# When the operands for the second token group are made, in a linear attention plus mixture-of-experts kernel on one core

## Chip, core and metric

One core of a Trainium2 chip runs the whole program. Its engines work side by side, each in the order of its own instruction list, and wait for one another by semaphores: PE (TensorE, matrix products; PEld is its weight load), DVE (VectorE), ACT (ScalarE), POOL (GpSimd) and SP (SyncE, which issues the DMAs). The metric is the device time of one execution in microseconds.

## The reference, cut to what matters

```
phi(x):  proj = x @ w_phi;  proj -= max|proj|;  return [exp(proj), exp(-proj)]
kv  = sum_s phi(k)_s v_s ;  z = sum_s phi(k)_s
attn = (phi(q) @ kv) / (phi(q) @ z + 1e-6)          # 4 batches, 8 heads, 576 tokens, width 64
x = attn as (2304 tokens, 512)
p = domain_probs / sum(domain_probs)
out = sum over 4 experts e of  p[:, e] * (relu(x @ w1[e]) @ w2[e])      # hidden width 1024
```

All is float32. Each matrix product on PE is made of three: both operands are split into a rounded part ("hi") and a remainder ("lo"), and lo*hi, hi*lo and hi*hi are added in PSUM.

## The kernel before, in words

**Work.** The attention runs over 16 pairs of heads (pair 15 is the last). The expert part runs over 48 units: a unit is two 128-wide slices of one expert's hidden width, for one group of tokens. Units 0 to 15 serve the first group (512 tokens, `first_units`, L623), 16 to 31 the second (1024 tokens), 32 to 47 the third (768 tokens). Units 16 to 47 (`strassen_unit`, L715) replace eight half-size products by seven, A to D, whose operands on the x side are B11, B21 (the x of the group's first half, already split) and T1, T2, T3, B22, T4, sums and differences of x blocks (`x_ops`, L664). A unit's second product is made of four tiles (eight in the second group) by `l2_tile` (L573); each ends with a DVE instruction "out" (L592) that adds the PSUM result into the output tile, and there are two PSUM buffers ("l"), so the third tile waits for the first tile's "out".

**Order.** The order in every engine's list is written out by the program. A heap holds functions with keys (`later`, L100); `tick` (L491) moves a clock on and runs what is due. From pair 4 on the attention of later pairs and the first group's units are interleaved. There a tick is one piece of three 128x512 matmuls on PE, and is worth 192/(256 x 0.88) = 0.852 of a key, from key 85 on. Unit 0 has 8 ticks and each later one 16: 8 for its own first product (L618), 8 for the second product of the unit before (L582). So unit 13 begins at tick 200 (key 255.5), unit 14 at 216, unit 15 at 232; the first group ends at tick 248 (key 296.4). Pair i's steps are listed in `STAGES` (L447) with keys 16i + offset: for pair 15 the last use of its inputs is at key 256 (L468), the denominators' reciprocal ("rec", L403) at 271.2, the multiplication by it (`x_mul`, L417, in place on the tile rb) at 276.9. `LAST` is 277. In the second group a tick is one product or tile, and the key moves by 1.

**The x operands before.** The second half of the second group's x lies in DRAM (xd), written by pairs up to 11. At key 280.7 (`to_late`, L883) the pool "att", which holds all attention tiles, is closed, and the pool "late" takes its place; `x_load` (L658) fetches 1 MB into the tile xr 1.5 ticks later. Then 32 functions are spread from 11 ticks on, 0.7 ticks apart: six DVE instructions make T1 = xr - hi - lo and T2 (L700 to L702), T2 is split (hi on ACT L685, lo on DVE L689), T1 is split (lo on POOL L689), two DVE instructions make T3 (L703), then T3 and B22 are split (lo on POOL), four DVE instructions make T4 (L704, L705), and it is split (lo on DVE). Each name stands for two instructions of 128x512, for the halves c = 0 and 1. Unit 16 issues a product only when its operand's functions have been issued (L782). In it, the four tiles of unit 15's second product all follow product A (L796).

**Beside them.** Units from 16 on need sums of weight blocks ("ws", four DVE instructions L522 to L525), their rounding on ACT (L541) and remainders on POOL (L549); weights of the second product are split by L506 (ACT) and L512 (POOL).

Of the kernel before, what the change touches and what calls it, by code (L numbers as in the profile page):

```python
# [11 lines left out]
F32 = mybir.dt.float32  # L12
F32R = mybir.dt.float32r
# [7 lines left out]
def kernel(  # L21
# [17 lines left out]
    P = 128  # L39
    B, NP = kq.shape[0], kq.shape[1]  # L40
    D = w_phi.shape[0]
    NF = w_phi.shape[1]
    S = kq.shape[3] // 2
# [4 lines left out]
    NPAIR = B * NP  # L48
# [5 lines left out]
    PER = 16  # L54
# [5 lines left out]
    COPY_ENG, COPY_ENG0 = "avvaaaa", "avaaaaa"  # L60
    LO_ENG, LO_ENG0, HI_ENG, HI_ENG0 = "vvvvgg", "vvvvgv", "vgg", "agg"

    XA_START, XA_GAP, XA_LATE, XA_LOAD = 11, 0.7, 3.7, 1.5
    FETCH = (12, 28, 40, 46)
    W_WAIT = (5.5, 4.0, 0, 3.5)

# [33 lines left out]
    def later(key, fn):  # L100
        heapq.heappush(queue, (key, next(count), fn))
# [5 lines left out]

    att_stack = ExitStack()
    ap_ = att_stack.enter_context(tc.tile_pool(name="att", bufs=2))
    wbd = ap_.tile([P, 2 * NF], F32, name="wbd", bufs=1)  # L110
    wbd_hi = ap_.tile([P, 2 * NF], F32R, name="wbd_hi", bufs=1)
    wbd_lo = ap_.tile([P, 2 * NF], F32R, name="wbd_lo", bufs=1)

    def v_tile(dtype, name, tag, mid):

        t = ap_.tile([P, 5, 192], dtype, name=name, tag=tag, bufs=2)
        nc.gpsimd.memset(t.bitcast(F32)[:, :, 64:P], mid)
        return t

# [10 lines left out]
    def load_pair(i, what):  # L130
        s = pairs[i]
        b, hp = divmod(i, NP)
        t0 = b * S
        if what == "kq":
            s.kq = [ap_.tile([P, 2 * S], F32, name="kq", tag="kq", bufs=2)]

            parts = ((0, 2 * P), (2 * P, 4 * P)) if i == 0 else ((0, 4 * P),)
            for a, z in (*parts, (S - 64, S), (S, S + 64), (S + 64, 2 * S)):
                to = a + {S - 64: 64, S: -64}.get(a, 0)
                nc.sync.dma_start(s.kq[0][:, to : to + z - a], kq[b, hp][:, a:z])  # L140
            return
        vsrc = v[t0 : t0 + S, hp * P : (hp + 1) * P]
        if s.split_kv:
            vraw = s.v = ap_.tile([P, 5, P], F32, name="vraw", tag="vraw", bufs=1)
            nc.sync.dma_start(vraw[:, 0:4, :], vsrc[0:512].rearrange("(t p) d -> p t d", p=P))
            for r0 in (0, 64):
                nc.sync.dma_start(vraw[r0 : r0 + 64, 4, :], vsrc[512:S])
            return
        s.v = (v_tile(F32, "v32", "vhi", 1.0),)
        nc.gpsimd.memset(s.v[0][0:64, 4, :], 0.0)  # L150
        for h in range(2):
            src, dst = vsrc[:, h * 64 : (h + 1) * 64], s.v[0][:, :, h * P : h * P + 64]
            nc.sync.dma_start(dst[:, 0:4], src[0:512].rearrange("(t p) d -> p t d", p=P))
            nc.sync.dma_start(dst[64:P, 4], src[512:S])
# [10 lines left out]
    def split_pair(i, what):  # L165
        s = pairs[i]
        if what == "v":
            if not s.split_kv:
                return
            hi, lo = v_tile(F32R, "vhi", "vhi", 1.0), v_tile(F32R, "vlo", "vlo", 0.0)  # L170
            for h in range(2):
                g, d = slice(h * P, h * P + 64), s.v[:, :, h * 64 : (h + 1) * 64]
                round_to(i, 2, hi[:, :, g], d)
                nc.gpsimd.tensor_tensor(
                    lo[:, :, g], d, hi[:, :, g].bitcast(F32), op=ALU.subtract
                )


            for h in range(2):
                g, d = slice(h * P, h * P + 64), s.v[0:64, 4, h * 64 : (h + 1) * 64]  # L180
                nc.gpsimd.tensor_scalar(lo[0:64, 4, g], d, 1.0, 0.0, op0=ALU.mult, op1=ALU.add)
            nc.gpsimd.memset(lo[0:64, 4, 64:P].bitcast(F32), 1.0)
            nc.gpsimd.memset(hi[0:64, 4, :].bitcast(F32), 0.0)
            s.v = (hi, lo)
            return
        if not s.split_proj:
            return
        raw = s.kq[0]
        sl = KSL if what == "k" else QSL
        n = sl.stop - sl.start  # L190
        hi = ap_.tile([P, n], F32R, name=f"{what}hi", tag=f"{what}hi", bufs=1)
        lo = ap_.tile([P, n], F32R, name=f"{what}lo", tag=f"{what}lo", bufs=1)
        round_to(i, "kq".index(what), hi, raw[:, sl])
        nc.gpsimd.tensor_tensor(lo, raw[:, sl], hi.bitcast(F32), op=ALU.subtract)  # L194
        setattr(s, what, (hi, lo))
# [19 lines left out]
    def proj_sub(i, what, c):  # L215

        s = pairs[i]
        g = 4 if c < 2 else 2
        n = g * NF
        m = ap_.tile([P, 4], F32, name="m", tag="m", bufs=4)  # L220
        psv = s.ps.pop((what, c))[:, :n].rearrange("p (g f) -> p g f", f=NF)
        nc.vector.tensor_reduce(m[:, :g], psv, axis=AX.X, op=ALU.max, apply_absolute_value=True)  # L222
        d = s.d[what, c] = ap_.tile([P, 512], F32, name="d", tag="d", bufs=3)
        nc.vector.tensor_tensor(  # L224
            d[:, :n].rearrange("p (g f) -> p g f", f=NF), psv,
            m[:, :g].unsqueeze(2).to_broadcast([P, g, NF]), op=ALU.subtract,
        )

    def exps(src, rows, g, n, split):

        if split:
            e = ap_.tile([P, 1024], F32, name="e", tag="e", bufs=2)
            hi = ap_.tile([P, 1024], F32R, name="ehi", tag="ehi", bufs=4)
        else:
            e = ap_.tile([P, 1024], F32, name="e32", tag="ehi", bufs=4)
        ev = e[rows, : 2 * g * n].rearrange("p (g s n) -> p g s n", s=2, n=n)
        nc.scalar.activation(ev[:, :, 0, :], src, AF.Exp)
        nc.scalar.activation(ev[:, :, 1, :], src, AF.Exp, scale=-1.0)
        if not split:
            return [e]  # L240
        sl = (rows, slice(0, 2 * g * n))
        nc.scalar.activation(hi[sl], e[sl], AF.Copy)  # L242
        return [hi, (e, sl)]
# [231 lines left out]
            later(PER * i + o, functools.partial(fn, i, *args))  # L475
    FIRST = PER * (NP - 1) + 37
    LAST = PER * (NPAIR - 1) + 37

# [2 lines left out]
    NU = NE * NFC // 2  # L483
    clock = Pair()
    weights = {}
    late = []

    def after(steps, fn, *args):
        later(clock.key + steps * clock.step, functools.partial(fn, *args))
# [25 lines left out]
    def s_sums(n):  # L515


        (raw,) = weights["w1", n]
        s = late[0].tile([P, 4, 256], F32, name="ws", tag="ws", bufs=1)
        a11, a12, a21, a22 = (raw[:, f, c * 256 : (c + 1) * 256] for f in range(2) for c in range(2))  # L520
        sub, tt = ALU.subtract, nc.vector.tensor_tensor
        tt(s[:, 0], a21, a22, op=ALU.add)  # L522
        tt(s[:, 1], s[:, 0], a11, op=sub)
        tt(s[:, 2], a11, a21, op=sub)
        tt(s[:, 3], a12, s[:, 1], op=sub)  # L525
        weights["w1", n] = (raw, s)
# [129 lines left out]
    )  # L656

    def x_load(x, first, nt, wait=0):  # L658
        raw = x.raw = late[0].tile([P, NP, 512], F32, name="xr", tag="xr", bufs=1)
        a = first * P  # L660
        src = xd[:, :, a : a + nt].rearrange("c p t -> p c t")
        after(wait, lambda: nc.sync.dma_start(raw[:, :, :nt], src))

    def x_ops(x):  # L664


        tt, sub, add = nc.vector.tensor_tensor, ALU.subtract, ALU.add
        b12, b22 = x.raw[:, 0:2, : x.nt], x.raw[:, 2:4, : x.nt]
        (hi1, lo1), (hi2, lo2) = ([t.bitcast(F32) for t in x.op[k]] for k in ("B11", "B21"))
        t = {"T3": b12, "B22": b22}  # L670

        def temp(name, c):
            if c == 0:
                t[name] = late[0].tile([P, 2, x.nt], F32, name=name, tag="tt", bufs=2)
            return t[name][:, c]

        parts = {}

        def hi(name, c):
            if c == 0:  # L680
                parts[name] = [
                    late[0].tile([P, 2, x.nt], F32R, name=f"{name}{k}", tag=f"{name}{k}", bufs=1)
                    for k in ("hi", "lo")
                ]
            nc.scalar.activation(parts[name][0][:, c], t[name][:, c], AF.Copy)  # L685
# [25 lines left out]
    def spread(ops, start, gap):  # L711
        for i, fn in enumerate(ops):
            after(start + gap * i, fn)
# [132 lines left out]
    with tc.manual_schedule():  # L846
# [26 lines left out]
        xa, xb = Pair(), Pair()  # L873
# [6 lines left out]
            }  # L880
        out1 = []

        def to_late():  # L883

            att_stack.close()
            late.append(ctx.enter_context(tc.tile_pool(name="late", bufs=1, reuse_waits="tile")))
            out1.append(late[0].tile([P, 4, DM], F32, name="out1"))
            x_load(xa, xa.first + 4, xa.nt, XA_LOAD)
            ops = x_ops(xa)
            spread(  # L890
                [fn for k in ("t", "T2", "T1", "t3", "T3", "B22", "t4", "T4") for fn in ops[k]],
                XA_START, XA_GAP,
            )

        later(LAST + XA_LATE, to_late)
        clock.key = FIRST
        clock.step = (LAST - FIRST) / (NU * (2 * NP + 2 * N0) * SPREAD)
        pend = first_units()
        clock.key = max(clock.key, LAST + XA_LATE)
        run_until(clock.key)  # L900
        clock.step = 1
        second_units(pend)


# [36 lines left out]
```

## Time and profile before

| what | value |
|---|---|
| median of 3 runs (lowest to highest) | 988.18 us (985.95 to 990.49) |
| the profiled execution, own time | 989.25 us |
| its span, first to last instruction | 987.5 us |
| mean granted TensorE clock | 0.993 of full speed |
| PE busy | 957.0 us (97%) |
| PEld busy | 823.0 us (83%) |
| DVE busy | 723.6 us (73%) |
| POOL busy | 582.2 us (59%) |
| ACT busy | 467.1 us (47%) |

The profiled execution is 1.07 us above the median. In the profile's view of 40 equal slices, PE is at 9 tenths nearly everywhere; after the first slice the lowest digits (8 and 7) are those of slices 16 and 17 of 40, where the first group of units gives way to the second. Starts and durations below are in us from the span's start; "[2.10 <-DVE out L592]" means that the engine had been idle for 2.10 us and that this instruction released it; "x2" that two like instructions were merged. In the views by stretch each engine has its busy time and, in brackets, its count of instructions; PEclk is the granted clock, 1.00 being full speed.

### The profile page before, as it was taken

To read this page: it belongs to the slowest core of one execution; us is meant where nothing else is said; L and a number is where in the kernel's file an instruction comes from. 1 tells how busy PE (TensorE), PEld (TensorE's weight loads), DVE (VectorE), ACT (ScalarE), POOL (GpSimd) and SP (SyncE) were. 2 spreads that over 40 slices of the span, in tenths; PEclk is the share of its full clock that TensorE was granted. 3 is DMA by queue.
4 is the path that set the end of the run, shared out by engine and by line. 5 is a ranking of instruction groups with operands and counts; after the bars stand their busy time and mean duration, and the time that the engine had idled before them with its cause. 6 is when DMAs were issued, how large, how long until landed. Compare 5 with 4: busy or idle time off the path is not lost. (4 is left out here: it accounts for less than half of the span.)

```text
span 987.5 us, 13367 instructions
## 1 busy us (share of the span) xinstructions
PE 957.0 (97%) x4871; PEld 823.0 (83%) x4871; DVE 723.6 (73%) x1026; ACT 467.1 (47%) x820; POOL 582.2 (59%) x487
## 2 busy tenths in 40 slices
PE   6999999999999998799999999999989999999998
PEld 5878888888888876688888888888878888888887
DVE  5588888898898757867666667668876667676764
ACT  4777666666676723424333333433434434343441
POOL 3588768778678345654555445544665565655651
PEclk9999999999999998999999999999999999999999
DMA  6433434334333243231121111221132221212211
GB/s 157 127 88 85 117 95 118 96 105 126 105 105 90 68 135 111 80 95 45 43 92 56 55 44 43 64 62 45 42 107 86 65 70 59 86 61 69 64 43 64
DMA packets 64273, 80.75 MB, mean 82 GB/s; under 512 B 20144, under 2 KB 29744, under 8 KB 64208
## 3 DMA queue, kind: packets, MB, share of 16 engines
q1 hardware_dynamic: 64208, 79.90, 27.2%
q8 instruction: 38, 0.62, 0.3%
q14 instruction: 27, 0.22, 0.1%
HBM read 72.40 MB, written 7.49 MB: 81 GB/s over the span
## 5 line engine op out<-in xcount | busy, mean ns | idle before, releaser
L592 DVE SCALAR_TENSOR_TENSOR out<-l,pr,out 128x512 f32<-128x512 f32 x270 | 200.5, 748 | 93.9 <-PE l L582 92.7
L582 PE MATMUL l<-w2hi,h_lo 128*128 128x512 f32 x576 | 227.8, 396 | 8.5 <-DVE out L592 8.4
L582 PE MATMUL l<-w2hi,h_hi 128*128 128x512 f32 x576 | 227.8, 395 | 0.0
L582 PE MATMUL l<-w2lo,h_hi 128*128 128x512 f32 x576 | 227.4, 395 | 0.0
L549 POOL TENSOR_TENSOR w1lo<-wraw,w1hi 128x512 fp32r<-128x512 f32 x64 | 78.2, 1242 | 99.7 <-ACT w1hi L541 62.0
L582 PEld LDWEIGHTS l<-w2hi,h_lo 128*128 128x128 f32 x576 | 109.1, 189 | 28.9 <-DVE out L592 11.2
L582 PEld LDWEIGHTS l<-w2hi,h_hi 128*128 128x128 f32 x576 | 109.1, 189 | 23.4
L582 PEld LDWEIGHTS l<-w2lo,h_hi 128*128 128x128 f32 x576 | 109.1, 189 | 17.5
L512 POOL TENSOR_TENSOR w2lo<-wraw,w2hi 128x1024 fp32r<-128x1024 f32 x48 | 116.3, 2423 | 11.5 <-ACT w2hi L506 7.9
L749 POOL TENSOR_TENSOR c<-u,s 128x512 f32<-128x512 f32 (+1 forms) x32 | 37.6, 1174 | 85.3 <-DVE u L736 85.3
L739 ACT ACTIVATE h_hi<-c 128x512 fp32r<-128x512 f32 (+1 forms) x96 | 54.9, 578 | 68.7 <-DVE c L736 67.7
L549 POOL TENSOR_TENSOR s_lo<-ws,s_hi 128x768 fp32r<-128x768 f32 x32 | 59.2, 1849 | 33.0 <-ACT s_hi L541 32.3
L765 ACT ACTIVATE c<-c 128x512 f32<-128x512 f32 (+1 forms) x32 | 18.5, 580 | 126.3 <-POOL c L749 126.3
L242 ACT ACTIVATE ehi<-e 128x1024 fp32r<-128x1024 f32 (+2 forms) x72 | 63.5, 882 | 2.3
L257 DVE TENSOR_TENSOR elo<-e,ehi 128x1024 fp32r<-128x1024 f32 x36 | 61.9, 1721 | 0.3 <-ACT ehi L242 0.2
L746 POOL TENSOR_TENSOR h_lo<-c,h_hi 128x512 fp32r<-128x512 f32 (+1 forms) x32 | 37.5, 1172 | 40.2 <-ACT h_hi L739 40.2
L194 POOL TENSOR_TENSOR klo<-kq,khi 128x640 fp32r<-128x640 f32 x15 | 27.2, 1815 | 49.7 <-ACT khi L163 15.7
L222 DVE TENSOR_REDUCE m<-proj 128x4 f32<-128x512 f32 (+1 forms) x80 | 50.5, 631 | 7.4 <-PE proj L210 6.8
L506 ACT ACTIVATE w2hi<-wraw 128x1024 fp32r<-128x1024 f32 x48 | 50.5, 1052 | 10.2 <-PE l L582 9.9
L736 DVE TENSOR_TENSOR u<-s,B 128x512 f32<-128x512 f32 (+1 forms) x32 | 19.9, 620 | 47.2 <-ACT s L733 24.1
L541 ACT ACTIVATE s_hi<-ws 128x768 fp32r<-128x768 f32 x32 | 27.1, 846 | 56.9 <-DVE ws L525 56.9
L224 DVE TENSOR_TENSOR d<-proj,m 128x512 f32<-128x512 f32 (+1 forms) x80 | 51.1, 638 | 3.6
(165 smaller groups left out, 2496.4 us busy)
## 6 DMA issues: line engine op xcount, KB each, us to landing
wraw<-in_w_dram SPq DMA_DIRECT2D x96, 512.0 KB, 3.9
kq<-in_kq_dram SPq DMA_DIRECT2D x31, 256.0 KB, 4.6
rb<-rec_d SPq DMA_DIRECT2D x32, 144.0 KB, 2.8
out_dram<-out SPq DMA_DIRECT2D x18, 256.0 KB, 2.0
vraw<-in_v_dram SPq DMA_DIRECT2D x12, 256.0 KB, 4.1
xd<-rb SPq DMA_DIRECT2D x8, 288.0 KB
xr<-xd SPq DMA_DIRECT2D x2, 768.0 KB
kq<-in_kq_dram SPq DMA_DIRECT2D x32, 32.0 KB, 3.3
```

The lines of the kernel that those rows point to most:

```text
L222: nc.vector.tensor_reduce(m[:, :g], psv, axis=AX.X, op=ALU.max, apply_absolute_value=True)
L224: nc.vector.tensor_tensor(d[:, :n].rearrange("p (g f) -> p g f", f=NF), psv, m[:, :g].unsqueeze(2).to_broadcast([P, g, NF]), op=ALU.subtract,)
L242: nc.scalar.activation(hi[sl], e[sl], AF.Copy)
L257: engine.tensor_tensor(lo[sl], e[sl], parts[0][sl].bitcast(F32), op=ALU.subtract)
L506: nc.scalar.activation(hi, raw, AF.Copy)
L512: nc.gpsimd.tensor_tensor(lo, raw, hi.bitcast(F32), op=ALU.subtract)
L549: nc.gpsimd.tensor_tensor(dst, src, hi.bitcast(F32), op=ALU.subtract)
L582: nc.tensor.matmul(ps, lhsT=l[:, f, j * P : (j + 1) * P], rhs=r[:, f, :], start=(f == 0 and k == 0), stop=(f == 1 and k == 2),)
L592: nc.vector.scalar_tensor_tensor(o, ps, p, o, op0=ALU.mult, op1=ALU.add)
L739: nc.scalar.activation(h[b][0][:, f, :nt], src, AF.Relu)
L746: nc.gpsimd.tensor_tensor(dst, src, hi.bitcast(F32), op=ALU.subtract)
L749: nc.gpsimd.tensor_tensor(temp("c22"), c["u3"], c["s5"], op=ALU.add)
```

## The change

A second pool for SBUF, "att_in", on the other side of the memory, takes those attention tiles that are last used by key 256: the projection's weights, kq, v, their parts, d and e. The pool is closed at key 256.1 (`LAST_IN`), and a pool "early" takes its place with xr, ws, the work tiles of T1, T2 and T4, and the parts of T1, T2 and T3. The load of xr is issued there, and the 20 functions of T1, T2 and T3 follow at keys 260.1, 261.1, ... 279.1, one per key. B22 and T4 stay in "late"; their 12 functions are issued from 0.5 ticks into unit 16 on, 0.45 ticks apart, a tick there being one key. (The diff leaves out five places where kq, vraw, the parts of k and q, d and e go from pool `ap_` to `ip_`, and nothing else.)

```diff
@@ -60,7 +60,7 @@
     COPY_ENG, COPY_ENG0 = "avvaaaa", "avaaaaa"
     LO_ENG, LO_ENG0, HI_ENG, HI_ENG0 = "vvvvgg", "vvvvgv", "vgg", "agg"
 
-    XA_START, XA_GAP, XA_LATE, XA_LOAD = 11, 0.7, 3.7, 1.5
+    X_IN, X_GAP, XA_START, XA_GAP, XA_LATE = 4, 1, 0.5, 0.45, 3.7
     FETCH = (12, 28, 40, 46)
     W_WAIT = (5.5, 4.0, 0, 3.5)
 
@@ -107,13 +107,17 @@
 
     att_stack = ExitStack()
     ap_ = att_stack.enter_context(tc.tile_pool(name="att", bufs=2))
-    wbd = ap_.tile([P, 2 * NF], F32, name="wbd", bufs=1)
-    wbd_hi = ap_.tile([P, 2 * NF], F32R, name="wbd_hi", bufs=1)
-    wbd_lo = ap_.tile([P, 2 * NF], F32R, name="wbd_lo", bufs=1)
+
+
+    in_stack = ExitStack()
+    ip_ = in_stack.enter_context(tc.tile_pool(name="att_in", bufs=2, side="right"))
+    wbd = ip_.tile([P, 2 * NF], F32, name="wbd", bufs=1)
+    wbd_hi = ip_.tile([P, 2 * NF], F32R, name="wbd_hi", bufs=1)
+    wbd_lo = ip_.tile([P, 2 * NF], F32R, name="wbd_lo", bufs=1)
 
     def v_tile(dtype, name, tag, mid):
 
-        t = ap_.tile([P, 5, 192], dtype, name=name, tag=tag, bufs=2)
+        t = ip_.tile([P, 5, 192], dtype, name=name, tag=tag, bufs=2)
         nc.gpsimd.memset(t.bitcast(F32)[:, :, 64:P], mid)
         return t
 
...
@@ -475,6 +479,7 @@
             later(PER * i + o, functools.partial(fn, i, *args))
     FIRST = PER * (NP - 1) + 37
     LAST = PER * (NPAIR - 1) + 37
+    LAST_IN = PER * (NPAIR - 1) + 16.1
 
 
 
@@ -483,7 +488,7 @@
     NU = NE * NFC // 2
     clock = Pair()
     weights = {}
-    late = []
+    early, late = [], []
 
     def after(steps, fn, *args):
         later(clock.key + steps * clock.step, functools.partial(fn, *args))
@@ -516,7 +521,7 @@
 
 
         (raw,) = weights["w1", n]
-        s = late[0].tile([P, 4, 256], F32, name="ws", tag="ws", bufs=1)
+        s = early[0].tile([P, 4, 256], F32, name="ws", tag="ws", bufs=1)
         a11, a12, a21, a22 = (raw[:, f, c * 256 : (c + 1) * 256] for f in range(2) for c in range(2))
         sub, tt = ALU.subtract, nc.vector.tensor_tensor
         tt(s[:, 0], a21, a22, op=ALU.add)
@@ -656,7 +661,7 @@
     )
 
     def x_load(x, first, nt, wait=0):
-        raw = x.raw = late[0].tile([P, NP, 512], F32, name="xr", tag="xr", bufs=1)
+        raw = x.raw = early[0].tile([P, NP, 512], F32, name="xr", tag="xr", bufs=1)
         a = first * P
         src = xd[:, :, a : a + nt].rearrange("c p t -> p c t")
         after(wait, lambda: nc.sync.dma_start(raw[:, :, :nt], src))
@@ -671,15 +676,16 @@
 
         def temp(name, c):
             if c == 0:
-                t[name] = late[0].tile([P, 2, x.nt], F32, name=name, tag="tt", bufs=2)
+                t[name] = early[0].tile([P, 2, x.nt], F32, name=name, tag="tt", bufs=2)
             return t[name][:, c]
 
         parts = {}
 
         def hi(name, c):
             if c == 0:
+                pool = (early if name in ("T1", "T2", "T3") else late)[0]
                 parts[name] = [
-                    late[0].tile([P, 2, x.nt], F32R, name=f"{name}{k}", tag=f"{name}{k}", bufs=1)
+                    pool.tile([P, 2, x.nt], F32R, name=f"{name}{k}", tag=f"{name}{k}", bufs=1)
                     for k in ("hi", "lo")
                 ]
             nc.scalar.activation(parts[name][0][:, c], t[name][:, c], AF.Copy)
@@ -880,18 +886,29 @@
             }
         out1 = []
 
+        xa_ops = {}
+
+        def to_early():
+
+            in_stack.close()
+            early.append(
+                ctx.enter_context(
+                    tc.tile_pool(name="early", bufs=1, side="right", reuse_waits="tile")
+                )
+            )
+            x_load(xa, xa.first + 4, xa.nt)
+            xa_ops.update(x_ops(xa))
+            fns = [fn for k in ("t", "T2", "T1", "t3", "T3") for fn in xa_ops[k]]
+            for i, fn in enumerate(fns):
+                later(LAST_IN + X_IN + X_GAP * i, fn)
+
         def to_late():
 
             att_stack.close()
             late.append(ctx.enter_context(tc.tile_pool(name="late", bufs=1, reuse_waits="tile")))
             out1.append(late[0].tile([P, 4, DM], F32, name="out1"))
-            x_load(xa, xa.first + 4, xa.nt, XA_LOAD)
-            ops = x_ops(xa)
-            spread(
-                [fn for k in ("t", "T2", "T1", "t3", "T3", "B22", "t4", "T4") for fn in ops[k]],
-                XA_START, XA_GAP,
-            )
-
+
+        later(LAST_IN, to_early)
         later(LAST + XA_LATE, to_late)
         clock.key = FIRST
         clock.step = (LAST - FIRST) / (NU * (2 * NP + 2 * N0) * SPREAD)
@@ -899,6 +916,7 @@
         clock.key = max(clock.key, LAST + XA_LATE)
         run_until(clock.key)
         clock.step = 1
+        spread([fn for k in ("B22", "t4", "T4") for fn in xa_ops[k]], XA_START, XA_GAP)
         second_units(pend)
 
 
```

## Rows read from the trace of the kernel before

**Rows 1.** Busy time by stretch, PE alone: stretch, busy (count), granted clock, DMA share, GB/s.
```profile
366.86:418.00 51.14, 40.19 (x154) 0.90 0.28 91
420.00:540.00 120.00, 120.00 (x531) 1.00 0.21 66
```

**Rows 2.** Timeline of PE: start, duration, line, what, idle time before and its releaser.
```profile
369.35 0.80 PE L582 MATMUL l<-w2hi,h_lo 128*128 128x512 f32 x1 [2.10 <-DVE out L592]
...
384.20 0.79 PE L582 MATMUL l<-w2hi,h_lo 128*128 128x512 f32 x1 [3.46 <-DVE out L592]
...
387.52 0.79 PE L582 MATMUL l<-w2hi,h_lo 128*128 128x512 f32 x1 [0.39 <-DVE out L592]
...
398.15 0.50 PE L582 MATMUL l<-w2hi,h_lo 128*128 128x512 f32 x1 [2.48 <-DVE out L592]
...
407.75 0.47 PE L787 MATMUL D<-T4hi,w1lo 128*128 128x512 f32 x1 [1.14 <-DVE u L736]
...
417.55 0.50 PE L787 MATMUL A<-x_hi,w1lo 128*128 128x512 f32 x1 [1.38 <-ACT s L733]
```

**Rows 3.** Busy time by stretch, PE alone, right behind three of these pauses.
```profile
368.90:372.50 3.60, 3.15 (x7) 0.55 0.84 244
384.00:389.80 5.80, 5.21 (x11) 0.50 0.29 90
398.00:401.00 3.00, 2.85 (x12) 1.00 0.47 170
```

**Rows 4.** Timeline of DVE, 379 to 403 us.
```profile
379.29 1.53 DVE L522 TENSOR_TENSOR ws<-wraw 128x256 f32<-128x256 f32 x1
...
382.80 0.68 DVE L700 TENSOR_TENSOR T<-xr,x_hi 128x512 f32<-128x512 f32 x1
383.40 0.74 DVE L592 SCALAR_TENSOR_TENSOR out<-l,pr,out 128x512 f32<-128x512 f32 x1
384.06 2.14 DVE L700 TENSOR_TENSOR T<-xr,x_hi 128x512 f32<-128x512 f32 x1
...
393.66 3.78 DVE L703 TENSOR_TENSOR xr<-xr 128x512 f32<-128x512 f32 x2
...
400.52 2.81 DVE L704 TENSOR_TENSOR T<-x_hi,T 128x512 f32<-128x512 f32 x2
```

**Rows 5.** Timeline of POOL, four instructions between 347 and 397 us.
```profile
347.60 2.39 POOL L512 TENSOR_TENSOR w2lo<-wraw,w2hi 128x1024 fp32r<-128x1024 f32 x1
...
353.12 2.41 POOL L512 TENSOR_TENSOR w1lo<-wraw,w1hi 128x1024 fp32r<-128x1024 f32 x1 [3.12 <-ACT w1hi L506]
...
383.83 1.82 POOL L549 TENSOR_TENSOR s_lo<-ws,s_hi 128x768 fp32r<-128x768 f32 x1 [1.57 <-ACT s_hi L541]
...
394.07 2.82 POOL L512 TENSOR_TENSOR w2lo<-wraw,w2hi 128x1024 fp32r<-128x1024 f32 x1
```

**Rows 6.** Timeline of DVE, 347 to 367 us.
```profile
347.76 0.48 DVE L295 TENSOR_SCALAR nd<-num,eps 128x256 f32<-128x256 f32 x1
349.19 2.20 DVE L422 TENSOR_TENSOR rb<-nd,rb 64x576 f32<-64x576 f32 x2 [0.94 <-DMA rb<-rec_d]
351.42 0.69 DVE L605 SCALAR_TENSOR_TENSOR h_lo<-l,h_hi 128x512 fp32r<-128x512 f32 x1
353.67 0.75 DVE L592 SCALAR_TENSOR_TENSOR out<-l,pr,out 128x512 f32<-128x512 f32 x1 [1.56 <-PE l L582]
...
358.44 0.21 DVE L403 RECIPROCAL rec<-den 128x9 f32<-128x9 f32 x1
...
366.00 2.51 DVE L422 TENSOR_TENSOR rb<-nd,rb 64x576 f32<-64x576 f32 x2 [0.68 <-DMA rb<-rec_d]
```

**Rows 7.** Timeline of SP: the last DMA issues before 345 us, and when the next follows.
```profile
334.86 0.34 SPq L398 DMA_DIRECT2D den<-den_d  x1
344.02 0.33 SPq L406 DMA_DIRECT2D rec_d<-rec  x1
```

**Rows 8.** The page's DMA issues: KB each, median us from issue to landing.
```profile
wraw<-in_w_dram SPq DMA_DIRECT2D x96, 512.0 KB, 3.9
```

**Rows 9.** Timeline of PE, 333 to 355 us: pair 15's last projection, unit 12's third tile.
```profile
333.58 0.28 PE L210 MATMUL proj<-wbd_hi,qhi 128*128 128x256 f32 x1
...
354.85 0.39 PE L582 MATMUL l<-w2hi,h_lo 128*128 128x512 f32 x1
```

More of the change, by code (lines that the diff above doesn't have):

```diff
@@ L134, in load_pair @@
         if what == "kq":
-            s.kq = [ap_.tile([P, 2 * S], F32, name="kq", tag="kq", bufs=2)]
+            s.kq = [ip_.tile([P, 2 * S], F32, name="kq", tag="kq", bufs=2)]
             parts = ((0, 2 * P), (2 * P, 4 * P)) if i == 0 else ((0, 4 * P),)
@@ L143, in load_pair @@
         if s.split_kv:
-            vraw = s.v = ap_.tile([P, 5, P], F32, name="vraw", tag="vraw", bufs=1)
+            vraw = s.v = ip_.tile([P, 5, P], F32, name="vraw", tag="vraw", bufs=1)
             nc.sync.dma_start(vraw[:, 0:4, :], vsrc[0:512].rearrange("(t p) d -> p t d", p=P))
@@ L190, in split_pair @@
         n = sl.stop - sl.start
-        hi = ap_.tile([P, n], F32R, name=f"{what}hi", tag=f"{what}hi", bufs=1)
-        lo = ap_.tile([P, n], F32R, name=f"{what}lo", tag=f"{what}lo", bufs=1)
+        hi = ip_.tile([P, n], F32R, name=f"{what}hi", tag=f"{what}hi", bufs=1)
+        lo = ip_.tile([P, n], F32R, name=f"{what}lo", tag=f"{what}lo", bufs=1)
         round_to(i, "kq".index(what), hi, raw[:, sl])
@@ L222, in proj_sub @@
         nc.vector.tensor_reduce(m[:, :g], psv, axis=AX.X, op=ALU.max, apply_absolute_value=True)
-        d = s.d[what, c] = ap_.tile([P, 512], F32, name="d", tag="d", bufs=3)
+        d = s.d[what, c] = ip_.tile([P, 512], F32, name="d", tag="d", bufs=3)
         nc.vector.tensor_tensor(
@@ L231, in exps @@
         if split:
-            e = ap_.tile([P, 1024], F32, name="e", tag="e", bufs=2)
+            e = ip_.tile([P, 1024], F32, name="e", tag="e", bufs=2)
             hi = ap_.tile([P, 1024], F32R, name="ehi", tag="ehi", bufs=4)
```

## The prediction, made before the result was known

> **What bounds the kernel now.** I read the page first: PE is busy 97% of the span, so a change elsewhere pays only where PE stands still. The busy time by stretch says where that is. From 420 to 540 us, in the steady second group, PE issues 531 matmuls in 120 us, 0.226 us each; from 366.86 to 418.00, where the first group ends, it issues 154 in 51.14 us [rows 1]. At 0.226 us those need 34.8 us, so 16.3 us are lost there, and this is all that a change of this passage can win. Next the timeline of PE: six pauses, 2.10, 3.46, 0.39, 2.48, 1.14 and 1.38 us, 10.95 us together, four of them ended by a DVE "out" [rows 2]. Behind two of them the granted clock is 0.55 and 0.50, which is the lower of its two levels (1.2 GHz), for 3.60 and 5.80 us; behind the pause of 2.48 us it is 1.00 [rows 3]. At the lower level half of the busy time is loss: 1.6 and 2.6 us. The remaining 1.1 us is the refilling of PE after the pauses.
>
> Then the timeline of DVE says why "out" is late. The pause until 384.20 ends after the "out" of 383.40, which stood behind the weight sums from 379.29 and one T1 instruction at 382.80; the pause until 398.15 follows the two T3 instructions, 3.78 us [rows 2, 4]. DVE instructions with two SBUF inputs vary here from 0.68 to 2.14 us for the same size [rows 4]. POOL explains it: the one of 384.06 took 2.14 us while POOL worked from 383.83 to 385.65, so it ended 0.55 us after POOL did [rows 4, 5]. The two halves of x_mul from 349.19 took 2.20 us, and POOL was busy until 349.99 [rows 5, 6]. So such a DVE instruction waits until the POOL instruction in hand is over. "out" and h_lo, which read PSUM, keep to 0.69 to 0.75 us [rows 6].
>
> The Trainium skill, "SBUF — State Buffer", section "Who interferes with whom", has the rule: a DVE instruction with two SBUF inputs and a GpSimd instruction that reads SBUF exclude each other, and whichever came first holds the other off entirely. That speaks against this change, which moves such DVE work to a place with long POOL instructions. The trace agrees for DVE; for POOL it shows 2.82 us instead of 2.41 beside T3's two instructions [rows 5], a delay.
>
> **The change part by part.** *The load.* xr takes the place of the projection's weights and kq, whose last reader, pair 15's last projection, starts at 333.58 [rows 9]. It goes into SP's list behind the issue at 334.86 and ahead of the one at 344.02 [rows 7], so SP, idle in between, can issue it at about 335.5 and nothing queued behind it waits. 512 KB land in 3.9 us [rows 8]; 1 MB needs 3.9 (if latency were all) to 7.8 us (twice the bytes). I take 7.8, landed by 343.5; the first T1 instruction comes after 347.76 [rows 6]. Cost 0; if the cover were gone, see the third rival.
>
> *Twenty instructions in pair 15's time.* Keys 260.1, 261.1, ... are ticks 206, 207, 208, 209, 211, 212 for T1 and T2, that is the end of unit 13's first product and the first tiles of unit 12's second. Ten of the twenty run on DVE, six on ACT, four on POOL. The steps of a T instruction and an "out" are, from start to start, 0.60 and 0.66 us [rows 4]. Now DVE's list: nd ends at 348.24; T1 c0 waits for POOL until 349.99 and ends at 350.6; x_mul, 1.4 us without POOL (2.20 less the 0.80 that it waited), 352.0; T1 c1, 352.6; h_lo, 353.2 [rows 5, 6]. POOL has begun w1lo at 353.12 and holds until 355.53 [rows 5]. T1's second step c0 and c1 are both ahead of "out" (tick 209 lies inside the first tile): 356.1 and 356.7, "out" at 357.4, which before was over at 354.42 [rows 6]. PE wants to begin the third tile at 354.85 [rows 9] and begins at 357.5: **a new pause, +2.65 us.** At the least, if DVE's pair slips past w1lo, it is +0.4; at the most POOL comes between the pair, again about 2.7.
>
> *The reciprocal.* Behind it DVE has T2 c0, "out", T2 c1, "out", the first T2 remainder, the fourth tile's "out" (PE ends that tile at 360.2, the "out" at 361.2), the second remainder, then rec: 361.8 instead of 358.44 [rows 6], 3.4 later, of which 2.65 is PE's own shift. Rec starts the DMA chain to x_mul at 366.00, and x_mul stands ahead of the "out" that ended the pause of 2.10 us [rows 2, 6]. **+0.7 us** (0 to 1.7, the latter if T3's subtraction waits for T1's remainder on POOL). ACT's six and POOL's four instructions lie where those engines have idle time; POOL delays weights used 15 us later. Cost 0 there; without that cover it would be one POOL instruction, 1.8 us [rows 5].
>
> *Taken away from 380 to 399.* The pause of 3.46 loses one T1 instruction, **-0.6**; the weight sums stay ahead of "out", so 2.9 remains (bounds: 0 to 0.6, nothing else there is moved). The pause of 0.39 goes with the T1 instruction of 2.14, **-0.4**. T3's 3.78 leave the pause of 2.48, but the four T4 instructions, issued at keys 298.7 to 300.05 of unit 16, now stand between the first and second "out" of unit 15's tiles. Before, two of them took 2.81 us [rows 4]. From the start a of product A the first tile ends at a+2.7, "out" at a+3.4, the four T4 at a+5.8 without POOL or a+7.2 with B22's remainders on it, the second "out" at a+6.5 to a+7.9, and the fourth tile is due at a+5.4. The pause becomes 1.1 to 2.5; I take 2.1, as POOL has work there: **-0.4**. The pause of 1.14 waits for u behind T4's first remainder, which is now earlier: **-0.6** (0 to 1.1). The pause of 1.38 is ACT's and stays.
>
> *The clock.* The new pause, 2.65, lies between 2.48 (no drop) and 3.46 (drop); nearest is 2.48, so I take 0 and keep 1.6 [rows 3] for the range.
>
> **Sum:** 2.65 + 0.7 - 0.6 - 0.4 - 0.4 - 0.6 = +1.35 us. On the profiled execution's 989.25 that is 990.6; that execution lies 1.07 above the median of 988.18, so the forecast for a median is **989.5 us**: pauses change places. By the page's rule in both directions POOL would be held off as well and T3's remainders would come about one instruction later before x_mul: +0.6, 990.1.
>
> **The rivals.** *One: DVE's pair slips past POOL and the passage gets shorter.* T1's pair escapes w1lo (0.1 us decides), rec is not late, and the pause at 384.20, now 2.9, no longer drops the clock: +0.4 - 0.6 - 0.4 - 2.6 - 0.6, and between -1.0 and -2.48 for the T3 pause: -4.8 to -6.3, about 982.6. For it: DVE has idle time of 0.94 and 1.56 in that stretch [rows 6]. Against: w1lo starts at 353.12 and lasts 2.41 [rows 5].
>
> *Two, slower: the clock.* If a pause of 2.65 is enough (one of 2.10 was [rows 2, 3]), the new pause costs 1.6 more; the T4 pause, at its 2.5 and with a drop as well, 0.4 + 1.9 more: +1.35 + 1.6 + 2.3 = +5.3, 993.4. It decides from a pause of some 2.1 to 2.6 us on.
>
> *Three: the load is late.* If xr has to wait for tiles that POOL reads until 347.60, it lands at 355.4 and DVE stands at T1 c0 with x_mul, h_lo and "out" queued behind: "out" at about 360.9, 3.5 later than in the forecast: +4.9, 993.0, and SP's issue of 344.02 [rows 7] would be held too. Against: the tiles freed first are the first to be used again.
>
> **How the numbers follow.** Forecast 0.55, rival one 0.25, two 0.15, three 0.05. A measurement of this kernel tells 0.5%, 4.9 us, from no change. Rival one lies beyond it (faster 0.25), two and three at or beyond it (slower 0.20), the forecast, whose own bounds taken together give 985 to 992, within it (0.55). The range, 982 to 994, reaches to the middle of rival one and takes in two and three.
>
> **What would show it.** Right: the same six or so pauses, a new one before unit 12's third tile (about 355 to 357.5) ended by "out", a T1 instruction of over 2 us beside w1lo, rec near 362, the pause before unit 14's third tile still near 3 us, no T instruction between 383 and 399 but T4's. Wrong: no pause at 355; the stretch from 366.86 on losing well under 12 us; xr landing after 348; or new pauses after 420, where I expect none.

## The result, and the profile after

The changed kernel takes **999.13 us** (median of 4 runs, 996.98 to 999.87), the kernel before, beside it on the same chip, 988.78 (4 runs, 985.95 to 990.49): a ratio of 1.0097, 95% interval [1.0071, 1.0122]. It is slower by 10.35 us, twice what a measurement can tell, where 989.5 had been forecast with a range of 982 to 994. Median and range are both missed.

The profiled execution is one of 999.87 us, 10.62 above the profiled one of before. Its page, the span, the engines' busy times and the granted clock by slice:

```profile
span 998.1 us, 13366 instructions
...
PE 963.6 (97%) x4871; PEld 826.2 (83%) x4871; DVE 724.3 (73%) x1026; ACT 467.2 (47%) x820; POOL 583.9 (58%) x487
...
PEclk9999999999999998899999999999999999999999
```

The work is the same: 4871 matmuls, DVE and POOL within 2 us of before. PE alone is busy 6.6 us longer, and a second slice has a lower clock. The timeline of PE after shows its pauses in the passage, in the form of [rows 2] (start, duration, idle time before and its releaser):

```profile
360.92 0.79 PE L587 MATMUL l<-w2hi,h_lo 128*128 128x512 f32 x1 [2.19 <-DVE out L597]
...
377.27 0.50 PE L587 MATMUL l<-w2hi,h_lo 128*128 128x512 f32 x1 [1.98 <-DVE out L597]
...
391.57 0.75 PE L587 MATMUL l<-w2hi,h_lo 128*128 128x512 f32 x1 [2.86 <-DVE out L597]
...
406.39 0.79 PE L587 MATMUL l<-w2hi,h_lo 128*128 128x512 f32 x1 [4.75 <-DVE out L597]
...
427.04 0.50 PE L793 MATMUL A<-x_hi,w1lo 128*128 128x512 f32 x1 [1.16 <-ACT s L739]
```

And PE by stretch right behind the first four, the columns as in [rows 3]:

```profile
360.00:363.50 3.50, 2.58 (x6) 0.63 0.05 10
376.00:381.00 5.00, 3.73 (x10) 0.70 0.15 59
391.00:396.00 5.00, 4.43 (x12) 0.66 0.30 105
406.00:412.00 6.00, 5.61 (x13) 0.50 0.53 157
```

The first pause is the new one that the prediction named, and it has a lower clock behind it. The fourth, where 2.1 us had been expected, is 4.75, with 13 matmuls at the lower clock. The pauses that ended at 387.52 and 407.75 before are gone.

**The account.** Both programs issue the same 4871 matmuls in the same order, so each can be put beside its like and its start in the one execution taken from that in the other. This shift, how much later the kernel after is, grows as follows, in us; the times are those of before unless marked as now:

| where | forecast | measured |
|---|---|---|
| 53 to 60 us, long ahead of the changed passage | 0 | +3.7 |
| new pause ahead of unit 12's third tile | +2.65 | +2.4 |
| clock behind it | 0 | +1.7 |
| rec later, x_mul ahead of "out" (pause now at 377.27) | +0.7 | +0.2 |
| pauses of 384.20 and 387.52, and the clock behind them | -1.0 | -2.0 |
| pause of 398.15, now at 406.39 | -0.4 | +2.3 |
| clock behind it | 0 | +2.7 |
| pauses of 407.75 and 417.55 | -0.6 | -1.5 |
| **the passage** (all lines so far but the first) | **+1.35** | **+5.8** |
| 420 to 726 us, no pause added | 0 | +2.3 |
| 726 us to the end, a clock drop in the kernel before alone | 0 | -1.2 |
| **whole** | **+1.35** | **+10.6** |

Five places make up most of the difference; the timelines show what happened at each. *T4.* First DVE, then POOL of the kernel after:

```profile
398.96 0.75 DVE L597 SCALAR_TENSOR_TENSOR out<-l,pr,out 128x512 f32<-128x512 f32 x1 [1.99 <-PE l L587]
399.63 2.70 DVE L710 TENSOR_TENSOR T<-x_hi,T 128x512 f32<-128x512 f32 x2
402.25 3.42 DVE L711 TENSOR_TENSOR T<-T,x_lo 128x512 f32<-128x512 f32 x2
405.60 0.74 DVE L597 SCALAR_TENSOR_TENSOR out<-l,pr,out 128x512 f32<-128x512 f32 x1
```

```profile
398.80 2.99 POOL L695 TENSOR_TENSOR B22lo<-xr,B22hi 128x512 fp32r<-128x512 f32 x2 [5.16 <-ACT B22hi L691]
401.74 2.78 POOL L517 TENSOR_TENSOR w2lo<-wraw,w2hi 128x1024 fp32r<-128x1024 f32 x1
```

POOL is busy without a break from 398.80 to 404.52, and the four T4 instructions, between two "out", need 6.1 us. Before, w2lo ran at 394.07 [rows 5], ahead of B22 and T4; the change issues B22's functions at unit 16's start, so in POOL's list the weights' remainder now stands behind them. Its own input, w2hi, was done at 397.32 on ACT, while POOL stood idle until 398.80 for B22hi.

*The new pause.* DVE and POOL after, at unit 12's second product:

```profile
351.87 2.40 DVE L706 TENSOR_TENSOR T<-xr,x_hi 128x512 f32<-128x512 f32 x1
354.20 1.53 DVE L426 TENSOR_TENSOR rb<-nd,rb 64x576 f32<-64x576 f32 x2
...
356.97 3.23 DVE L707 TENSOR_TENSOR T<-T,x_lo 128x512 f32<-128x512 f32 x2
360.12 0.74 DVE L597 SCALAR_TENSOR_TENSOR out<-l,pr,out 128x512 f32<-128x512 f32 x1
```

```profile
351.32 2.41 POOL L517 TENSOR_TENSOR w2lo<-wraw,w2hi 128x1024 fp32r<-128x1024 f32 x1
...
356.66 2.39 POOL L517 TENSOR_TENSOR w1lo<-wraw,w1hi 128x1024 fp32r<-128x1024 f32 x1 [2.93 <-PE num L377]
```

T1's second step starts 0.3 us behind the start of w1lo, and the "out" behind it comes late, as forecast.

*The early part* lies where the change touches no instruction's order. The first fence is DVE before, the second DVE after, the third POOL after:

```profile
52.69 0.75 DVE L422 TENSOR_TENSOR rb<-nd,rb 64x576 f32<-64x576 f32 x1 [0.62 <-DMA rb<-rec_d]
53.60 1.19 DVE L422 TENSOR_TENSOR rb<-nd,rb 64x576 f32<-64x576 f32 x1 [0.16 <-DMA rb<-rec_d]
```

```profile
53.72 4.60 DVE L426 TENSOR_TENSOR rb<-nd,rb 64x576 f32<-64x576 f32 x2 [1.21 <-DMA rb<-rec_d]
```

```profile
55.36 2.33 POOL L517 TENSOR_TENSOR w2lo<-wraw,w2hi 128x1024 fp32r<-128x1024 f32 x1
```

The DMA that x_mul waits for landed about 1 us later, so the second half was still in hand when unit 1's w2lo began, and it ended after w2lo did. Before, it was over by 54.8.

*From 420 to 726.* The pace of the matmuls themselves differs. PE after: six products on x, six on T2 and the next tile's first, each run's first line:

```profile
440.84 0.39 PE L793 MATMUL A<-x_hi,w1lo 128*128 128x512 f32 x1
...
442.20 0.39 PE L793 MATMUL B<-T2hi,s_lo 128*128 128x512 f32 x1
...
443.60 0.39 PE L587 MATMUL l<-w2hi,h_lo 128*128 128x512 f32 x1
```

The same in the kernel before:

```profile
431.28 0.39 PE L787 MATMUL A<-x_hi,w1lo 128*128 128x512 f32 x1
...
432.64 0.39 PE L787 MATMUL B<-T2hi,s_lo 128*128 128x512 f32 x1
...
434.00 0.39 PE L582 MATMUL l<-w2hi,h_lo 128*128 128x512 f32 x1
```

On x: 1.36 us for six in both, 0.227 each. On T2: 1.40 after (0.233) and 1.36 before. No pause shows it; the count of matmuls in a long stretch does. The first line is before, the second after:

```profile
440.00:700.00 260.00, 260.00 (x1149) 1.00 0.19 57
```

```profile
440.00:700.00 260.00, 260.00 (x1139) 1.00 0.19 59
```

Ten matmuls fewer in 260 us, at a full clock and no idle time.

*From 726 on.* Ahead of the third group's first product PE pauses equally long in both executions. Only the kernel before has the lower clock behind it. The pause and the stretch behind it, first before, then after:

```profile
726.27 0.44 PE L787 MATMUL A<-x_hi,w1lo 128*128 128x384 f32 x1 [2.56 <-ACT s L733]
```

```profile
726.00:730.00 4.00, 3.73 (x13) 0.71 0.58 223
```

```profile
738.09 0.44 PE L793 MATMUL A<-x_hi,w1lo 128*128 128x384 f32 x1 [2.55 <-ACT s L739]
```

```profile
737.80:741.80 4.00, 3.71 (x19) 1.00 0.60 231
```

So 1.5 us of the comparison go the other way, with no work of the change in it.

### The profile page after: what moved, and what is told of

Read it like the earlier page. It is cut to its first block, busy times and chain, and to the rows that moved or that the text cites. A ratio compares the mean times of both kernels' runs of the same rounds, so it can differ in the third digit from the quotient of the medians.

```text
span 998.1 us, 13366 instructions
## 1 busy us (share of the span) xinstructions
PE 963.6 (97%) x4871; PEld 826.2 (83%) x4871; DVE 724.3 (73%) x1026; ACT 467.2 (47%) x820; POOL 583.9 (58%) x487
## 5 line engine op out<-in xcount | busy, mean ns | idle before, releaser
L198 POOL TENSOR_TENSOR klo<-kq,khi 128x640 fp32r<-128x640 f32 x15 | 27.2, 1812 | 49.5 <-DMA wraw<-in_w_dram 13.7
```

## The experiments

The theory taken into them: the slowdown is made of DVE held up by POOL at two places (T1's second step, T4), the clock behind those pauses, and the place of T1 to T3 in SBUF. The rivals: that the new pool or the earlier load costs by itself, that a late T1 would only move the wait, and that the place is innocent. Ratios are against the kernel before, with its median from the runs that shared the chip.

**The two pools alone.** The operands' functions and the load go back to where they were; the pools stay, and with them the place of T1 to T3's parts within 4096 bytes.

```diff
-            x_load(xa, xa.first + 4, xa.nt)
-            xa_ops.update(x_ops(xa))
-            fns = [fn for k in ("t", "T2", "T1", "t3", "T3") for fn in xa_ops[k]]
-            for i, fn in enumerate(fns):
-                later(LAST_IN + X_IN + X_GAP * i, fn)
...
+            x_load(xa, xa.first + 4, xa.nt, 1.5)
+            ops = x_ops(xa)
+            spread(
+                [fn for k in ("t", "T2", "T1", "t3", "T3", "B22", "t4", "T4") for fn in ops[k]],
+                11, 0.7,
+            )
...
-        spread([fn for k in ("B22", "t4", "T4") for fn in xa_ops[k]], XA_START, XA_GAP)
```

> The two pools as in the changed kernel, but the load of xr and all 32 functions issued where the kernel before issues them. Theory A (the loss is made of pauses and lower clock between 355 and 412 us; the 3.7 us that the changed kernel is already late at 60 us are chance in the arrival of DMAs): within 2 us of the kernel before, about 988 to 991. Theory B (the tiles' new places cost time wherever they are used): about 4 to 5 us over the kernel before, 993, with the 3.7 us at 60 us there again.

Measured: 991.35 us (10 runs), before 989.82; ratio 1.0033 [1.0012, 1.0053]. In its profile the passage costs 0.3 us, the early part is late as in the changed kernel, and the stretch of 440 to 700 us holds 1139 matmuls again. The time is as theory A had it, the late early part as theory B. So the pools cost about 1.5 us (1.2 to 5.2 by the interval) without any operand being made earlier, and the slow pace comes with them, not with the order. The greater part of the 10 us is the order's. The profiled execution is the slowest of the ten, 996.04, 4.7 us above their median: what it shows of the early part need not hold for the others.

**T4 behind the tiles.** Unit 15's tiles all come first, then B22 and T4.

```diff
-    X_IN, X_GAP, XA_START, XA_GAP, XA_LATE = 4, 1, 0.5, 0.45, 3.7
+    X_IN, X_GAP, XA_START, XA_GAP, XA_LATE = 4, 1, 6.3, 0.45, 3.7
```

> The changed kernel with XA_START 6.3 in place of 0.5, so that the four T4 instructions on DVE come behind the fourth out of unit 15's tiles. Theory A: the pause of 4.75 us and the 2.4 us at the lower clock behind it go, and at most 1 us comes back before product D; 5 to 7 us less than the changed kernel, 992 to 994. Rival (the pause belongs to something else, such as the weights' remainder on POOL): pause and time as in the changed kernel, 998 to 1000.

Measured: 990.4 us (10 runs); 1.0006 [0.9985, 1.0027]. One constant gives back 8.7 us: the pause near 400 is gone, and the passage is 3.6 us shorter than before the change. Behind the pause at 361 the clock stayed up here, although the edit comes 30 us after it. Pause and stretch in this kernel:

```profile
360.95 0.50 PE L587 MATMUL l<-w2hi,h_lo 128*128 128x512 f32 x1 [2.48 <-DVE out L597]
```

```profile
360.50:363.50 3.00, 2.55 (x11) 1.00 0.06 7
```

A pause of 2.48 us without a drop, where one of 2.19 had it in the kernel after: in this region the length alone does not decide, and in the profiled executions 1.7 us of the gain are not this edit's doing.

**T4 where it is, POOL out of its way.** This tells whether T4's four instructions are too many for their place or POOL makes them so: B22 goes behind the tiles, unit 16's w2lo is cut into four, T4 stays.

```diff
+        if kind == "w2" and n == 16:
+            for f in range(2):
+                for z in (slice(0, 256), slice(256, 512)):
+                    nc.gpsimd.tensor_tensor(
+                        lo[:, f, z], raw[:, f, z], hi[:, f, z].bitcast(F32), op=ALU.subtract
+                    )
+        else:
...
-        spread([fn for k in ("B22", "t4", "T4") for fn in xa_ops[k]], XA_START, XA_GAP)
+        spread([fn for k in ("t4", "T4") for fn in xa_ops[k]], 2.3, XA_GAP)
+        spread(xa_ops["B22"], 6.3, XA_GAP)
```

> The changed kernel with T4's functions where they are, between the first and second out of unit 15's tiles, but B22's functions behind the tiles and the w2lo that followed them on POOL made as four. Theory A (of the pause of 4.75 us some 3.5 are waits for POOL): T4's four DVE instructions take 2.6 to 3.8 us instead of 6.1, the pause falls to 1.2 to 2.4 us; 3 to 6 us less than the changed kernel, 993 to 996. Rival (four more instructions ahead of out are enough): pause over 4 us and time within 1.5 us of the changed kernel.

Measured: 992.3 us (10 runs); 1.0036 [1.0016, 1.0057]. DVE in this kernel, then the pause on PE and the clock behind it:

```profile
396.16 1.77 DVE L717 TENSOR_TENSOR T<-x_hi,T 128x512 f32<-128x512 f32 x2
397.85 1.28 DVE L718 TENSOR_TENSOR T<-T,x_lo 128x512 f32<-128x512 f32 x2
```

```profile
399.84 0.50 PE L594 MATMUL l<-w2hi,h_lo 128*128 128x512 f32 x1 [1.67 <-DVE out L604]
```

```profile
399.60:402.60 3.00, 2.76 (x12) 1.00 0.27 97
```

The four take 3.05 us instead of 6.1, the pause falls from 4.75 to 1.67, and the clock stays. So T4's term was sound for a free POOL, and POOL's order was the cause: w2lo ran from 393.94, 2.2 us ahead of T4's first instruction. B22's move and the cut of w2lo were not tried apart. Its median stays above that of the version that moves T4 away (992.3 against 990.4), which fits the pause that is left.

**T1's second step later.** All but the first two of the twenty functions come 3 keys later, past the "out" they held up.

```diff
-                later(LAST_IN + X_IN + X_GAP * i, fn)
+                later(LAST_IN + X_IN + X_GAP * i + (3 if i > 1 else 0), fn)
```

> The changed kernel with all but the first two of the 20 functions three keys later, so that T1's second step comes behind the second out of unit 12's tiles and no longer beside POOL's remainder of unit 15's first weights. Theory A: the pause of 2.19 us at 361 and the 1.7 us at the lower clock behind it go; about 4 us less than the changed kernel, 995, with at most 1 us more before unit 13's last tile. Rival (any ten more DVE instructions delay the tiles here): the pause moves to the next tile and the time stays within 1.5 us of the changed kernel.

Measured: 998.03 us (4 runs); 1.0087 [1.0054, 1.0119]. Against the changed kernel that is 1.1 us less, too little to tell from none. The pause at 361 and its clock drop are gone, and the next has grown. PE and DVE in this kernel:

```profile
375.38 0.80 PE L587 MATMUL l<-w2hi,h_lo 128*128 128x512 f32 x1 [4.91 <-DVE out L597]
```

```profile
371.80 1.54 DVE L426 TENSOR_TENSOR rb<-nd,rb 64x576 f32<-64x576 f32 x2 [3.25 <-DMA rb<-rec_d]
373.37 1.29 DVE L709 TENSOR_TENSOR xr<-xr 128x512 f32<-128x512 f32 x2
374.58 1.40 DVE L597 SCALAR_TENSOR_TENSOR out<-l,pr,out 128x512 f32<-128x512 f32 x2
```

T3's two instructions now stand behind x_mul, which waits for its DMA, and ahead of both "out". The rival was right: the wait moves, because DVE's list runs strictly in order and x_mul blocks whatever is behind it.

**Unit 15's w1lo in four.** The order stays; POOL's one instruction of 128x1024 becomes four of 128x256, by the same loop as above under `kind == "w1" and n == 15`.

> The changed kernel with that one POOL instruction (unit 15's w1lo, 128x1024, 2.4 us) made as four of 128x256. Theory A, by way of DVE waiting for the POOL instruction in hand: T1's second step takes about 0.6 us per instruction more instead of 1.9 for the first, the pause at 361 falls below 1.3 us and the clock stays up; 2.5 to 4 us less than the changed kernel, 995 to 996.5. Rival (the number of DVE instructions ahead of out makes the pause): pause and time within 1 us of the changed kernel.

Measured: 996.07 us (4 runs); 1.007 [1.0045, 1.0095]. DVE, then POOL:

```profile
352.68 2.29 DVE L714 TENSOR_TENSOR T<-T,x_lo 128x512 f32<-128x512 f32 x2
```

```profile
352.54 3.71 POOL L520 TENSOR_TENSOR w1lo<-wraw,w1hi 128x256 fp32r<-128x256 f32 x4 [3.09 <-ACT w1hi L511]
```

T1's pair takes 2.29 us instead of 3.23 and POOL 3.71 instead of 2.39: they alternate. The new pause falls from 2.19 to 1.25 and its clock drop goes, while the next pause grows from 1.98 to 3.23, so the passage gains only 1.0 us. The rest of the 3.1 us between the medians is not shown to be this edit's: in its profiled execution the early part is not late (-0.2 us at 60 us, where the changed kernel has +4.2). By the Trainium skill, "SBUF — State Buffer", section "Who interferes with whom", the issue order decides who blocks, and a DVE instruction with two SBUF inputs contends with a GpSimd instruction that reads SBUF; both traces here agree, since shorter POOL instructions shortened DVE's wait.

**The place of T1 to T3.** As the program places them, their parts begin 32 bytes ahead of a multiple of 4096 in each partition after the change, and 1056 bytes behind one before. Their pool ends at a fixed place, with the tile ws last in it, so a longer ws moves them down: by 3008 bytes to 1056 as before, or by 64 bytes.

```diff
-        s = early[0].tile([P, 4, 256], F32, name="ws", tag="ws", bufs=1)
+        s = early[0].tile([P, 1024 + 752], F32, name="ws", tag="ws", bufs=1)
+        s = s[:, 0:1024].rearrange("p (a b) -> p a b", b=256)
```

(The second kernel has 16 in place of 752.)

> The changed kernel with 3008 bytes more per partition behind ws, so that every tile of the pool early begins 1056 bytes past a multiple of 4096, as T1, T2 and T3 did before, and not 32 bytes ahead of one. Theory A (the place of the operand sets the pace: between 440 and 700 us matmuls on T1, T2, T3 take 233 ns in the changed kernel and 227 before, those on B22 and T4 227 in both): 227 ns again, 2 to 2.5 us less than the changed kernel, 996.5 to 997.5. Rival (the second pool's side of the memory, or the pool itself, is slow): 233 ns stay and the time is that of the changed kernel, 998 to 1000.

> The same with 64 bytes: the tiles begin 4000 bytes past a multiple of 4096, that is 32 past a multiple of 128 as before and not 96. If the place within 128 bytes matters: 227 ns. If what matters is a larger block: 233 ns still, or something between for some of the tiles.

Measured: with 3008 bytes 995.09 us (6 runs), before 989.62; 1.0066 [1.0043, 1.0089]. With 64 bytes 998.51, a single run. The six products on T2 in the kernel with 3008, then the stretch of 440 to 700 us in each of the two:

```profile
438.74 0.39 PE L794 MATMUL B<-T2hi,s_lo 128*128 128x512 f32 x1
...
440.10 0.39 PE L588 MATMUL l<-w2hi,h_lo 128*128 128x512 f32 x1
```

```profile
440.00:700.00 260.00, 260.00 (x1149) 1.00 0.19 59
```

```profile
440.00:700.00 260.00, 260.00 (x1141) 1.00 0.20 59
```

With 3008 bytes six take 1.36 us and the count is that of before; with 64 bytes the pace stays slow (0.232 us each on T1 to T3). So the place sets the pace, and it is the place that cost 2.3 us. Which property of it does is open: three places were seen. The other 1.7 us between this kernel's median and that of the changed one are not the place's, as far as the profile tells: in its execution the early part is 1.9 us less late, and the pause at 359.02, as long as in the changed kernel (2.19), has no clock drop behind it.

**Put together, and once more past T3.** T4 behind the tiles, the 3008 bytes, and unit 15's w1lo in four; then the same with T3's six functions 10.4 keys later (and the added bytes as a tile of their own behind T3's parts).

```diff
-                later(LAST_IN + X_IN + X_GAP * i, fn)
+                later(LAST_IN + X_IN + X_GAP * i + (10.4 if i > 13 else 0), fn)
```

> T4 behind the tiles, 3008 bytes behind ws, and unit 15's w1lo as four instructions, together. If the three are independent: 990.4 less 2.2 less 1.5 to 3, 985 to 987, 3 to 5 us less than the kernel before. If the pauses only change places (what is won at unit 12's tiles is lost before x_mul's): 988 to 989.

> The same with T3's six functions 10.4 keys later, in unit 15's first product, behind x_mul. Theory A: x_mul no longer meets T3's remainders on POOL, the pause before unit 13's last tile shrinks by 1 to 1.5 us; 984 to 986. Rival: T3's subtraction then meets POOL's work there and the pause before unit 14's third tile, 2.86 us, grows by as much: time as the run before it.

Measured: 985.41 us (12 runs), 0.997 [0.9952, 0.9987], and 986.52 (12 runs), 0.9977 [0.9956, 0.9998], before 989.62. The three repairs together bring 13.7 us against the changed kernel and turn its loss into a gain of 4. T3 later brings nothing: the pause before unit 14's third tile grows from 2.86 to 5.19 us.

**The early part.** Unit 1's w2lo in four (the same loop under `kind == "w2" and n == 1`), in the changed kernel, in the kernel before, and in the joined version.

> The changed kernel with one POOL instruction far ahead of the change, w2lo of unit 1 (128x1024, 55.4 us), made as four of 128x256. Theory A (the 3.7 us at 60 us arise when x_mul's second half comes just behind this instruction's start): matmuls at 60 us under 1.5 us later than in the profile before, and 2 to 4 us less than the changed kernel, 995 to 997. Rival (the DMAs themselves or the new places of the tiles make it): still 3 to 4 us late at 60 us, time unchanged within 1.5 us.

> The kernel before with the same w2lo in four. If the kernel before is caught there in some executions too, its slower ones go: median 0.5 to 2 us less than the kernel before, highest run under 991. If only the new pools bring x_mul there: no difference within 0.5 us.

> T4 behind the tiles, 3008 bytes behind ws, and both long POOL instructions (unit 15's w1lo, unit 1's w2lo) in four. Theory A: 1.5 to 3.5 us less than the same without the early one (985.4), 982 to 984. Rival: as that run, 985 to 986.5.

Measured, beside 989.86 for before (30 runs): changed kernel 996.13 (7 runs), 1.0069 [1.0043, 1.0095]; before 987.7 (12 runs), 0.998 [0.9962, 0.9998]; joined version **982.92** (12 runs), 0.9941 [0.9919, 0.9963]. All three medians fall against the same kernel without the cut, by 3.0, 2.2 and 2.5 us. Each is near the limit of what these runs can tell (the intervals of the first and the third overlap those without the cut), and the mechanism is not shown. In the profiled execution of the first, PE is about 3 us late all the same. DVE, then POOL, in it:

```profile
53.59 4.01 DVE L426 TENSOR_TENSOR rb<-nd,rb 64x576 f32<-64x576 f32 x2 [2.52 <-DMA rb<-rec_d]
```

```profile
53.43 2.77 POOL L520 TENSOR_TENSOR w2lo<-wraw,w2hi 128x256 fp32r<-128x256 f32 x4
```

DVE waited 2.52 us for rb, POOL ran its four pieces back to back in 2.77 us, and x_mul's first half, begun 0.16 us behind the first piece, ended after the last; unlike T1's pair beside w1lo, DVE did not get in between. When it does is open, and so is why rb's DMA lands at times 1 us later. Of the 12 profiles with the two pools 10 are late by 2.3 to 4.5 us at 60 us; that of unit 15's w1lo in four and that of the joined version are not, nor are the two with the old pools. The profile of the kernel before with the cut gains nothing there: its execution is 1.7 us shorter by clock drops that are missing near 369 and 726 us, so where that median's 2.2 us come from is open too.

The joined version beats both kernels: 6.9 us under before, 16.2 under the changed one. It keeps the change's gain after 384, while its pauses at 355.02 (0.79) and 370.26 (1.99) stay.

## Why the prediction was wrong

**The step that failed is T4's**, in "Taken away from 380 to 399": "the four T4 at a+5.8 without POOL or a+7.2 with B22's remainders on it". That is 2.4 to 3.8 us for the four; they took 6.1. I had moved B22's remainders in POOL's list and left out what this pushes back: w2lo, 2.78 us, which before had run at 394.07 and now stands behind B22, beside T4's second pair. So a forecast of -0.4 became +2.3, and +2.7 more at the lower clock. With POOL out of the way the pause was 1.67, inside the stated 1.1 to 2.5.

**The clock's term** was set at 0 because 2.65 lay nearest to a pause of 2.48 without a drop. The new pause, 2.19, had one in the kernel after (+1.7) and none in two kernels with the same pause. The trace of before already had a nearer case, which the prediction did not read: the pause of 2.56 at 726.27, with a drop. Such a pause has no sure price. Later than 30 us the 14 profiles hold 33 pauses of 1.87 to 2.56 us; 16 have the lower clock behind them and 17 do not, so it should have stood as a half chance in the sum. Behind T4's pause the drop (+2.7) follows from the first error: every pause of 2.86 and more in the passage, in all these kernels, shows a drop. The second rival, "the clock", had both places right. That its +5.3 for the passage is close to the 5.8 measured is in part luck: it priced T4's pause and drop at +1.9, where they cost 5.0, and the other pauses took off more than it allowed. Its 993.4 missed for what lies outside the passage.

**What had no term at all**: the operands' place in SBUF (+2.3) and the early part. Both lie outside the passage, which the prediction called "all that a change of this passage can win"; that bounds a gain, but a change can lose time elsewhere. New tiles move operands that PE reads for 300 us. The early part is +3.7 between the two profiled executions. How much of it belongs to the difference of the two kernels, and how much to the executions that happened to be profiled, is open.

**What held.** The new pause: +2.4 for +2.65, by the instruction and the POOL instruction named. The pause of 3.46 kept 2.86 of the forecast 2.9. No T instruction stands between 383 and 399 but T4's. The pause at 407.75 went. The load cost nothing, though not for the reason given: SP issued it not at 335.5 but 8.6 us later,

```profile
344.07 0.37 SPq L667 DMA_DIRECT2D xr<-xd  x1
```

which is about 340 once the early 3.7 us are taken off; its place had also been that of v's parts, which pair 15's kv products read until 340 before, and SP waited 5.1 us for those. The transfer was over by 349, and T1 started at 351.87 with DVE not idle before it. The reciprocal's +0.7 did not come: rec is 8.4 us later than before (366.81), of which 7.8 are PE's own shift by then, and the pause it was to lengthen is 1.98 after 2.10.

## What to carry over

When a step is moved to an engine's free time, write out that engine's whole list behind it: what now stands behind the moved instructions, and who waits for that, cost more here than the moved work itself. DVE instructions with two SBUF inputs should not stand ahead of an instruction that frees a PSUM buffer while a long POOL instruction is due; moving T4's behind the tiles and cutting the POOL instruction beside T1's paid 13.7 us here together with the operands' place. Moving T1's alone did not pay, since the wait moved to the next "out". And when tiles move, count matmuls in a long stretch without pauses: a pace that differs by 1% appeared in no wait. Last, two profiled executions of two kernels differ by more than the change: here some clock drops came and went by themselves, so a comparison wants more than one profile of each.

## What the runs showed of the hardware that was not expected

The pace of matmuls of 512 columns depended on where the operand of T1 to T3 begins in SBUF: 227 ns at 1056 bytes behind a multiple of 4096, 233 ns at 32 bytes ahead of one, 232 ns at 96 bytes ahead, all at a granted clock of 1.00. Of 33 pauses of 1.87 to 2.56 us, 16 were followed by the lower clock (the shortest 1.97), at some 1.5 to 1.7 us each, and 17 were not (the longest 2.56); one of 3.12, near 59 us with the 3008 bytes, was not either. And four short POOL instructions let DVE in between in one place (3.71 us for the four, DVE's pair 2.29) and held it off to their end in another (2.77 and 4.01).
